# Reading 64 bytes of each row of the first keys and values from ScalarE's queue, ahead of all loads

## The chip, the cores and the metric

The kernel runs on one core of a Trainium2 chip. The metric is the device time of one execution in microseconds (us); lower is better. A core has five engines that run side by side, each with its own instruction stream: TensorE (PE, with the weight loads shown apart as PEld), VectorE (DVE), ScalarE (ACT), GpSimd (POOL) and SyncE (SP). Transfers between the chip's memory and the core's on-chip memory are made by 16 DMA engines. SP, ACT and POOL can issue them, each into a queue of its own.

## The reference

Three stages follow one another, all in float32 (inputs of 8 batches, 8 heads, 576 positions, 64 channels):

```python
a = softmax(phi, axis=2)                       # (8, 8, 576, 32)
k_m = einsum('bhsm,bhsd->bhmd', a, k)          # keys and values summed
v_m = einsum('bhsm,bhsd->bhmd', a, v)          # into 32 memory rows
attn = softmax(q @ k_m.T / 8)
x = (attn @ v_m), heads side by side           # (4608, 512)

logits = x @ moe_phi                           # (4608, 32): 8 experts x 4 slots
slot_input = softmax(logits, axis=0).T @ x
slot_out[e] = relu(slot_input[e] @ w1[e]) @ w2[e]
y = softmax(logits, axis=1) @ slot_out

h = y @ w_in                                   # (4608, 2048)
out = softplus(h) @ w_out                      # (4608, 512)
```

## The kernel before

The host lays the inputs out so that each load is one transfer over 128 partitions. The keys and values of a batch stand in one array `kv[b]` of 128 rows of 18,432 bytes; `phi[b]` has 128 rows of 4,608 bytes, `q[b]` 128 rows of 8,192 bytes.

The order of the work on every engine is written out ahead of time by a small planner in the kernel (`Flow`): generators yield units of work with an assumed duration and the tokens they need, and the planner lists them in one fixed order per engine. It also puts products of a zero tile (`idle`, line 937) into TensorE's stream wherever it expects TensorE to wait; their number and place are fixed when the program is built, and are not changed by what happens on the chip.

There are three stages in time:

- Attention, batch by batch (until about 125 us): loads of `phi`, `kv`, `q`; softmax over the memory rows (`memory_softmax`, DVE line 443, ACT line 447), transposes (line 465), the sums of keys and values (`memory_kv`, line 510), scores, token softmax, logits.
- The experts (about 125 to 177 us): SP streams in `moe_w1` and `moe_w2` (lines 1038 and 1052, tile `w`), TensorE uses each as it comes (lines 1250 and 1283).
- The last two products (177 us to the end): dense TensorE work (line 1795 above all), with the output stored on the way.

All loads are issued by SP, in one fixed order:

```python
def load_kv(b):                                              # lines 400-411
    n = KV + KVL
    parts = (slice(0, n), slice(n, n + KV)) if b == 0 else (slice(0, n + KV),)
    for i, c in enumerate(parts):
        ...
        nc.sync.dma_start(out=kv_t[b][:, c], in_=kv[b][:, c])    # line 409

def attention_loads():                                       # lines 428-436
    yield from load_phi(0)                                       # line 397
    yield [("D", 0.1)], [], 0
    nc.sync.dma_start(out=mphi..., in_=moe_phi)                  # line 431
    for b in range(B):
        yield from load_kv(b)
        if b + 1 < B:
            yield from load_phi(b + 1)
        yield from load_q(b)
```

So SP's order is phi(0), moe_phi, kv(0) in two parts of 10,240 and 8,192 bytes a row, phi(1), q(0), kv(1), phi(2), q(1), and so on. The loads report to eight completion counters in turn, so that each load waits in SP's stream for the one eight places before it; a load also waits until its place in on-chip memory is free. After the attention loads come the first weights `wi`, `wo` of the last stage, the expert weights, and further `wi` and `wo`.

ACT issues no transfer in this kernel. Its stream begins with the loading of an activation table (line 337), and its first computing instruction is the exponential of line 447.

Of the kernel before, what the change touches and what calls it, by code (L numbers as in the profile page):

```python
# [10 lines left out]
F32 = mybir.dt.float32  # L11
# [267 lines left out]
def tile_slot_attention_soft_moe_softplus_mlp(  # L279
# [13 lines left out]
    nc = tc.nc  # L293
# [28 lines left out]
    const = ctx.enter_context(tc.tile_pool(name="const", bufs=1))  # L322
# [11 lines left out]
    SX = room[:, :1152].rearrange("p (k s) -> p k s", k=KC)  # L334
    c_all = room[:, 1152:].rearrange("p (c s) -> p c s", s=NS)

    nc.scalar.preload_act_table_set("natural_log_exp_and_others")
    make_identity(nc, ident)

# [1660 lines left out]
```

## Time and profile before

| | |
|---|---|
| median of 3 runs | 575.95 us (573.95 to 576.41) |
| the profiled execution | 574.74 us |
| its span, first to last instruction | 573.0 us |
| mean granted TensorE clock | 0.997 |
| moved by DMA | 133.63 MB, mean 233 GB/s |

The profile is taken in one execution. Its span leaves 1.74 us of that execution's time outside. The busy time of an engine is an average over stages with different limits, so the rows below are taken by stage. A chain of waits is followed back from the last instruction to whatever released it. In rows on windows, an engine's busy time is in us with the number of instructions, the granted clock is a share of full speed, and DMA share is the busy share of the 16 DMA engines.

### The profile page before, as it was taken

The page shows a single profiled execution, that of the slowest core. Times are in us where ns is not written, and L with a number is a line of the kernel's source. Part 1 is how long each engine was busy: PE and PEld are TensorE (multiplying, and loading weights), DVE is VectorE, ACT ScalarE, POOL GpSimd, SP SyncE. Part 2 cuts the span into 40 slices and gives each one's busy share as a digit, 9 for nine tenths or more (in the row PEclk, how much of TensorE's full clock was granted, in tenths as well). Part 3 has the DMA queues.
Part 4 walks back from the last instruction along what each step waited for, and adds up shares of the span by engine and source line. Part 5 has one row for each costly group of instructions (what it writes and reads, how often), then busy time and mean ns, then how long its engine had stood idle before and what let it go on. Part 6 is the DMA issues. An engine that isn't in the chain of part 4 may idle for free.

```text
span 573.0 us, 10068 instructions
## 1 busy us (share of the span) xinstructions
PE 544.8 (95%) x4039; PEld 415.8 (73%) x4046; DVE 449.8 (79%) x568; ACT 372.9 (65%) x527; POOL 89.7 (16%) x107
## 2 busy tenths in 40 slices
PE   8888998889879999999999999999999999999997
PEld 4566764445536788888788888887888878888885
DVE  3677865749835999999999999999989837787953
ACT  3677674433433797588969876877796976775520
POOL 1021212410000011001032121231212310211100
PEclk9999999999999999999999999999999999999999
DMA  8999999999999458467778975899578774665832
GB/s 314 422 418 424 414 420 428 421 428 415 426 416 420 191 143 226 163 187 172 253 184 158 154 131 98 152 165 172 103 134 148 128 134 69 116 114 114 165 82 110
DMA packets 25103, 133.63 MB, mean 233 GB/s; under 512 B 3296, under 2 KB 4960, under 8 KB 18784
## 3 DMA queue, kind: packets, MB, share of 16 engines
q1 hardware_dynamic: 15120, 96.81, 42.0%
q0 software_dynamic: 9936, 36.18, 36.5%
q8 instruction: 32, 0.52, 0.4%
q14 instruction: 15, 0.12, 0.1%
HBM read 85.00 MB, written 44.04 MB: 225 GB/s over the span
## 4 chain that ended last, share of the span: by engine, by line
PE 84%; DVE 6%; DMA 5%; ACT 3%; issue 1%; POOL 0%; SPq 0%; POOLq 0%; DVEq 0%; ACTq 0%
PE ob L1795 52%; PE ob L1655 8%; DMA w<-in_moe_w_dram 5%; PE hp L1682 5%; PE idle L937 3%; PE kvp L510 3%; PE hid L1250 2%; PE rp L590 1%; PE sc L629 1%; PE tp L465 1%; DVE s L636 1%; PE S L1283 1%; DVE smx L634 1%; PE ob L1823 1%; ACT a L609 1%
## 5 line engine op out<-in xcount | busy, mean ns | idle before, releaser
L1795 PE MATMUL ob<-g,WS 128*128 128x512 f32 x768 | 181.2, 389 | 0.0
L1795 PEld LDWEIGHTS ob<-g,WS 128*128 128x128 f32 x768 | 144.1, 188 | 30.1 <-issue 0.2
L1795 PE MATMUL ob<-g,W 128*128 128x512 f32 x552 | 130.7, 390 | 1.5 <-ACT outs L818 1.3
L1795 PEld LDWEIGHTS ob<-g,W 128*128 128x128 f32 x552 | 103.4, 188 | 24.1 <-ACT outs L818 2.7
L818 ACT ACTIVATE outs<-ob 128x1024 f32<-128x1024 f32 x81 | 83.1, 1026 | 56.1 <-PE ob L1795 47.7
L1444 POOL DMA_DIRECT2D out_dram<-outs x63 | 57.2, 935 | 330.7 <-DVE outs L1437 101.2
L1748 DVE TENSOR_TENSOR g<-arena,g 128x1024 fp32r<-128x1024 f32 x55 | 66.6, 1221 | 26.3 <-ACT g L1746 26.1
L1746 ACT ACTIVATE g<-arena 128x1024 fp32r<-128x1024 f32 x55 | 58.0, 1056 | 17.1 <-PE ob L1795 12.8
L1655 PE MATMUL ob<-g,W 128*128 128x512 f32 x192 | 46.9, 391 | 0.2 <-ACT outs L818 0.2
L1655 PEld LDWEIGHTS ob<-g,W 128*128 128x128 f32 x192 | 35.8, 188 | 8.2 <-ACT outs L818 0.6
L1748 DVE TENSOR_TENSOR g<-room,g 128x1024 fp32r<-128x1024 f32 x29 | 35.2, 1221 | 5.0 <-ACT g L1746 4.8
L1682 PE MATMUL hp<-CT,Gs 128*128 128x512 f32 x128 | 38.3, 390 | 0.0
L1437 DVE TENSOR_TENSOR outs<-ob,outs 128x1024 f32<-128x1024 f32 x27 | 33.0, 1222 | 6.2 <-PE ob L1795 6.0
L1748 DVE TENSOR_TENSOR g<-x,g 128x1024 fp32r<-128x1024 f32 x28 | 34.0, 1220 | 4.8 <-ACT g L1746 4.7
L1746 ACT ACTIVATE g<-room 128x1024 fp32r<-128x1024 f32 x29 | 30.4, 1056 | 4.8 <-PE ob L1795 4.8
L1746 ACT ACTIVATE g<-x 128x1024 fp32r<-128x1024 f32 x28 | 29.6, 1056 | 3.9 <-PE ob L1795 2.3
L937 PE MATMUL idle<-zero 128*128 128x512 bf16 x96 | 26.5, 413 | 2.3 <-POOL zero L940 1.5
L683 POOL TENSOR_TENSOR a<-s,ssm 128x512 f32<-128x512 f32 (+1 forms) x20 | 18.8, 961 | 62.5 <-DVE r L482 24.3
L1695 ACT ACTIVATE arena<-hp 128x1024 f32<-128x1024 f32 x28 | 27.4, 1018 | 1.3 <-DVE g L1748 1.3
L1682 PEld LDWEIGHTS hp<-CT,Gs 128*128 128x128 f32 x128 | 23.9, 188 | 5.3 <-DVE gq L1386 0.2
L1283 PE MATMUL S<-w,hT 128*32 128x256 f32 x256 | 15.8, 381 | 4.2 <-ACT hT L1269 2.1
L510 PE MATMUL kvp<-kv,et 128*32 128x128 f32 x512 | 19.1, 283 | 0.7 <-DMA kv<-in_kv_dram 0.7
(197 smaller groups left out, 734.3 us busy)
## 6 DMA issues: line engine op xcount, KB each, us to landing
out_dram<-outs POOLq DMA_DIRECT2D x63, 512.0 KB, 5.4
w<-in_moe_w_dram SPq DMA_DIRECT2D x15, 2048.0 KB, 18.1
kv<-in_kv_dram SPq DMA_DIRECT2D x7, 2304.0 KB, 25.2
out_dram<-outs SPq DMA_DIRECT2D x20, 512.0 KB, 3.9
q<-in_q_dram SPq DMA_DIRECT2D x8, 1024.0 KB, 21.6
wi<-in_w_in_dram SPq DMA_DIRECT2D x8, 1024.0 KB, 19.0
wo<-in_w_out_dram SPq DMA_DIRECT2D x8, 1024.0 KB, 15.3
phi<-in_phi_dram SPq DMA_DIRECT2D x8, 576.0 KB, 19.5
```

The lines of the kernel that those rows point to most:

```text
L510: nc.tensor.matmul(kvp[32 * h : 32 * h + 32], lhsT=rows[:, 32 * h : 32 * h + 32], rhs=rows_of[:, c, h] if c < SC else rest[:, h], start=(c ...
L818: nc.scalar.activation(o, i, AF.Copy)
L937: nc.tensor.matmul(idle[0], lhsT=zero[:, :128], rhs=zero, start=True, stop=True)
L1283: nc.tensor.matmul(S2[half][32 * i : 32 * i + 32], lhsT=hT_t[e][:, kc8 % 2, kc8 // 2], rhs=w2_t[e, kb][:, half, i], start=(n == 0), stop=( ...
L1437: nc.vector.tensor_tensor(out=o, in0=OB[at], in1=o, op=ALU.add)
L1444: nc.gpsimd.dma_start(out=place(half, tb), in_=o, accum_op=ALU.add)
L1655: nc.tensor.matmul(bank(oc), lhsT=W[u][:, w, i, c], rhs=hb[tb, u][:, x, i], start=(fresh and i == chunks[0] and k == "0"), stop=(stop and ...
L1682: nc.tensor.matmul(hp[:, i], lhsT=Gs[:, 128 * fc : 128 * fc + 128], rhs=CTf[:, TB * tb : TB * tb + TB], start=True, stop=True,)
L1695: nc.scalar.activation(X[key][:, m], hp, AF.Softplus)
L1746: nc.scalar.activation(g[:, 0], x, AF.Copy)
L1748: nc.vector.tensor_tensor(out=g[:, 1], in0=x, in1=g.bitcast(F32)[:, 0], op=ALU.subtract)
L1795: nc.tensor.matmul(OB[at][:, t], lhsT=(W if w == "W" else WS)[u][:, x, c, cols], rhs=g[:, y, m], start=(fresh and u == grp[0] and n == 0), ...
```

## The change

A tile of 64 bytes a partition is added, and ACT's first instruction becomes a transfer that reads the first 64 bytes of each of the 128 rows of `kv[0]` into it. Nothing reads the tile. It stands in front of the table load in ACT's stream. Tiles placed after it in on-chip memory move up by 64 bytes. The transfer takes its turn on the eight completion counters, ahead of SP's loads.

```diff
@@ -334,6 +334,8 @@
     SX = room[:, :1152].rearrange("p (k s) -> p k s", k=KC)
     c_all = room[:, 1152:].rearrange("p (c s) -> p c s", s=NS)
 
+    touched = const.tile([128, 16], F32, name="touched")
+    nc.scalar.dma_start(out=touched, in_=kv[0][:, :16])
     nc.scalar.preload_act_table_set("natural_log_exp_and_others")
     make_identity(nc, ident)
```

## Rows read from the trace of the kernel before

**Rows 1.** The page: busy time of the engines, and the chain that ended last.

```profile
PE 544.8 (95%) x4039; PEld 415.8 (73%) x4046; DVE 449.8 (79%) x568; ACT 372.9 (65%) x527; POOL 89.7 (16%) x107
...
PE 84%; DVE 6%; DMA 5%; ACT 3%; issue 1%; POOL 0%; SPq 0%; POOLq 0%; DVEq 0%; ACTq 0%
```

**Rows 2.** Windows from the first transfer to the last expert weight.

```profile
core 0: us, PE busy (x) PEld busy (x) DVE busy (x) ACT busy (x) POOL busy (x), PEclk, DMA share, GB/s
...
1.70:2.50 0.80, 0.80 (x3) 0.30 (x2) 0.72 (x2) 0.32 (x1) 0.80 (x4) 1.00 0.89 230
2.50:3.60 1.10, 1.10 (x4) 0.33 (x3) 1.09 (x2) 0.00 (x0) 0.81 (x1) 1.00 0.99 377
3.60:7.20 3.60, 3.60 (x11) 1.29 (x10) 1.81 (x4) 1.56 (x4) 0.00 (x0) 1.00 0.90 246
7.20:12.00 4.80, 4.80 (x26) 2.52 (x25) 0.50 (x3) 0.35 (x2) 0.00 (x0) 1.00 0.98 410
12.00:60.00 48.00, 42.44 (x745) 30.16 (x745) 33.94 (x59) 32.19 (x82) 7.41 (x8) 0.96 1.01 422
...
100.00:147.00 47.00, 42.91 (x550) 23.78 (x550) 35.16 (x75) 19.03 (x44) 7.44 (x9) 1.00 1.00 422
147.00:173.00 26.00, 19.48 (x263) 10.46 (x268) 14.28 (x22) 9.63 (x20) 0.00 (x0) 1.00 1.00 421
```

**Rows 3.** The chain of waits, 140 to 180 us: start, us, what.

```profile
147.05 28.23 DMA w<-in_moe_w_dram
...
175.33 0.64 PE S L1283 x8
```

**Rows 4.** TensorE's waits, 150 to 176 us: us in total, times, longest.

```profile
PE S L1283 <- DMA w<-in_moe_w_dram: 2.0, 3, 0.7
PE hid L1250 <- DMA w<-in_moe_w_dram: 1.2, 2, 0.9
```

**Rows 5.** TensorE's waits, 176 us to the end.

```profile
PE ob L1795 <- ACT outs L818: 1.3, 2, 1.1
PE ob L1655 <- ACT outs L818: 0.2, 1, 0.2
```

**Rows 6.** The timeline of the start: start, us, engine, line, operation.

```profile
0.74 1.28 ACT L337 ACT_TABLE_LOAD   x1 [0.74 <-PEq L1984]
...
0.75 0.37 SPq L397 DMA_DIRECT2D phi<-in_phi_dram  x1
...
1.47 9.77 PE L937 MATMUL idle<-zero 128*128 128x512 bf16 x32 [1.47 <-POOL zero L940]
1.65 0.91 SPq L409 DMA_DIRECT2D kv<-in_kv_dram  x2
...
3.56 1.54 SPq L409 DMA_DIRECT2D kv<-in_kv_dram  x1
...
4.25 1.35 DVE L443 TENSOR_REDUCE nmx<-phi 128x2 f32<-128x1152 f32 x1 [0.16 <-DMA phi<-in_phi_dram]
5.14 0.62 SPq L397 DMA_DIRECT2D phi<-in_phi_dram  x1
...
6.41 0.76 ACT L447 ACTIVATE phi<-phi,nmx 128x576 f32<-128x576 f32 x1
...
11.07 0.60 PE L465 MATMUL tp<-ident,phi 128*128 128x128 f32 x4
...
12.47 0.65 PE L510 MATMUL kvp<-kv,et 128*32 128x128 f32 x16
```

**Rows 7.** DMA issues in the first 30 us: count, KB each, us to landing.

```profile
kv<-in_kv_dram SPq DMA_DIRECT2D x1, 1280.0 KB, 8.4
...
mphi<-in_moe_phi_dram SPq DMA_DIRECT2D x1, 64.0 KB, 3.2
```

## Prediction

> **What bounds the kernel now.** I read the page first, then the windows by stage, then the chain of waits around the place where the stages meet, and last the timeline of the first microseconds, where the change acts.
>
> The page makes it look like a TensorE kernel: TensorE is busy 95% of the span and holds 84% of the chain that ended last, the transfers only 5% [rows 1]. That 5% is one piece: the chain goes through a transfer of expert weights that was issued at 147.05 us and landed 28.23 us later, and the product of line 1283 that waited for it starts at 175.33 us [rows 3]. Before that moment the stage is bound by the DMA engines. From 12 us to 173 us their share is 1.00 to 1.01 at 421 to 422 GB/s in every window shown [rows 2]: the queue never runs dry, and the last expert weight lands when all bytes ahead of it have been moved, whenever they were issued. TensorE's high busy time in the first 60 us includes products of a zero tile (line 937) and hides this. From 150 to 176 us TensorE waits five times for weights, 2.0 + 1.2 = 3.2 us in total [rows 4]; it is ready before they are. After 176 us it waits 1.3 + 0.2 = 1.5 us in all, for ScalarE [rows 5]; it is the bound to the end.
>
> So a microsecond gained or lost in the DMA stream anywhere before 175 us arrives at the end nearly whole, up to about the 3.2 us that TensorE has in hand, and one gained on another engine in the start arrives nowhere.
>
> The stream does not start at its full rate. Against 421 GB/s, the windows lose: 1.7 to 2.5 us at 230 GB/s, 0.8 × (1 − 230/421) = 0.36 us; 2.5 to 3.6 us at 377, 0.11 us; 3.6 to 7.2 us at 246, 1.50 us; 7.2 to 12 us at 410, 0.13 us [rows 2]. The sum is 2.1 us. The large term is the third. By bytes, the windows up to 3.6 us have moved 0.18 + 0.41 = 0.60 MB, which is phi(0) (128 × 4,608 bytes = 0.59 MB); moe_phi is 0.07 MB; so from 3.6 us on the stream is in the first part of kv(0). The DMA engines are not idle there (share 0.90): they are slow at what they do.
>
> **The change part by part.**
>
> *The issue on ACT.* SP's issues at the start take 0.37 us to 1.54 us for one transfer [rows 6]. ACT's will take something between, most likely 0.4, and the table load of 1.28 us behind it then ends near 0.74 + 0.4 + 1.28 = 2.4 us, at the latest 0.74 + 1.54 + 1.28 = 3.6 us. What is queued behind it is the exponential of phi(0), which waits for the maximum that VectorE begins at 4.25 us and needs 1.35 us for [rows 6]. The cover is 2.0 us even in the worst case; cost 0. Without that cover, ACT would be late by the difference, and then TensorE's transposes of line 465.
>
> *The transfer itself.* It moves 128 pieces of 64 bytes, 8 KB. At the stream's rate that is 0.02 us. No row shows pieces this small; the nearest is moe_phi, 128 pieces of 512 bytes, 64 KB, 3.2 us from issue to landing [rows 7], whose bytes take 0.16 us of the stream at 421 GB/s. I take 0.05 us between them, nearer the row than the bytes alone would be; both ends stay.
>
> *Its effect on phi(0).* Both are issued near 0.75 us, so the first rows of phi(0) share the DMA engines with it. If phi(0) is later, the maximum of 4.25 us and the exponentials (the second ends at 6.41 + 0.76 = 7.2 us) are later. TensorE comes to phi(0) at 11.07 us, after 32 zero products that it runs in any case [rows 6]. The cover is 3.9 us. Cost 0 in this chain.
>
> *Its effect on kv(0).* The first product on it starts at 12.47 us [rows 6]; the first part was issued at 1.65 us and landed 8.4 us later, at 10.05 us [rows 7]. An earlier landing is worth nothing to TensorE, a later one up to 2.4 us costs it nothing. What counts is the stream behind: kv(0) at full rate lets every later byte go earlier. This is the one term with weight. From below: nothing, if the slow 3.6 us have nothing to do with these rows being read for the first time, or if the small pieces are as slow and hold the same DMA engines. From above: the 1.50 us of the third window. For a gain speaks that phi(0) had just run at 377 GB/s when kv(0) began at 246: the stream was already up, and fell again at this array [rows 2]. Against it speaks that new rows of the same array (kv(0) needs 0.66 + 1.31 = 1.97 MB from the start for its first part, and only about 1.48 MB were moved by 7.2 us), and then q(0), kv(1) and all weights, run at 410 to 422 GB/s at their first reading [rows 2]. A price that is paid once for a stretch of the array, and not by each row, fits both. I take half of the bound, 0.75 us.
>
> In the stream that makes −0.75 + 0.05 = −0.70 us.
>
> The Trainium skill bears on the half (DMA: Bandwidth & Descriptors, section "Issuing engines are not separate DMA queues"): it says that transfers started by different engines run on the same 16 DMA engines and interleave, so a queue of its own saves only issue time. By it ScalarE's queue is no way around: a piece that is slow occupies an engine that phi(0) needs, and the sum would be near +0.05 us. The window that would agree, phi(0) beside another queue, is not in this trace.
>
> *The counters and the addresses.* With the new transfer first in turn, SP's eighth load, phi(2), has it as predecessor. It was issued at 5.14 us [rows 6]; if the new transfer lands by the 3.2 us of moe_phi [rows 7], at 0.75 + 3.2 = 3.95 us, nothing waits. If it were 1.5 us later, phi(2) would be issued 0.3 us late behind kv(1), whose own 2.4 MB need 5.6 us of stream: 0. The shift by 64 bytes changes no instruction; no row prices it, and I take 0 and keep a small chance for new waits (below).
>
> **The sum.** Profiled execution: 574.74 − 0.70 = 574.04 us. That execution lay 1.21 us under the median of the runs, within their spread; on the median it is 575.95 − 0.70 = 575.25, say 575.2 us.
>
> **The rivals.**
>
> *Nothing moves* (0.33). The slow 3.6 us belong to the start of the stream, or their price is paid by the small pieces on the same DMA engines just before. For it: full rate at the first reading of everything later. Against it: the fall from 377 to 246 [rows 2]. Time: 575.95 + 0.02 to 0.16, so 576.0 us. The Trainium skill has a rule that would put the slowness down to load (same page, section "Latency and other measured facts": a memory access takes 0.2 us on average and 2 us at high load). By it a reading at the quiet start would prepare nothing, and the time is this rival's. The trace speaks against it in so far as the load is higher after 12 us, where the rate is full.
>
> *The price is paid twice* (0.14, the other side). The pieces are the first on the DMA engines and as slow as kv(0) is in rows 2, so phi(0) stands behind them for up to 1.50 us, and what 64 bytes prepare does not hold for the other 18,368 of a row. Price: 1.50 + 0.16 = 1.66 us, 577.6 us. It decides as soon as the delay before phi(0) is larger than what is saved after 3.6 us. Against it: phi(0) is itself a first reading, and lost only 0.36 us.
>
> *The whole start is mended* (0.10). All 1.50 us of the third window and the 0.36 us of the first go: 575.95 − 1.86 = 574.1 us.
>
> *Something else moves* (0.08): a new wait from shifted addresses, or TensorE's clock. It was granted 0.96 on average from 12 to 60 us [rows 2], where the stream covers it; half of these cases to each side.
>
> **How the numbers follow.** The forecast, a gain of 0.3 to 1.2 us, has 0.35; it is the likeliest, at 575.2 us. The medians of three runs scatter too: the three shown span 2.5 us. The cases reach from 574.1 to 577.6 us; I leave out the ends of the outer two and add the scatter: 573.6 to 577.3 us. A measurement of this kernel tells about 0.5%, 2.9 us, from no change. The whole slow start is worth 2.1 us and the price paid twice 1.66 us, so no case but the last reaches that by itself; scatter adds a little. Faster 0.07, same 0.86, slower 0.07.
>
> **What would show it.** In the profile after: the window 3.6 to 7.2 us well over 246 GB/s with 1.7 to 3.6 us not lower by as much; kv(0) landing under 8.4 us; the last product of line 1283 starting at about 174.6 instead of 175.33 us; and the span shorter by the same amount. If the first windows lose what the third gains, the first rival holds. If line 1283 starts earlier and the span does not shorten, my step from 175 us to the end is wrong. A new wait in front of the exponential at line 447, or of SP's loads, would make the covers wrong.

## The result, and the profile after

The changed kernel takes 581.43 us (median of 7 runs, 578.24 to 583.85); the kernel before took 575.11 us in the same comparison (7 runs, 573.69 to 578.27). The ratio is 1.0094, 95% interval 1.0069 to 1.0118: slower by about 0.9%. The profiled execution took 581.61 us with a span of 579.8 us and a mean granted clock of 0.985, against 573.0 us and 0.997 before. Lines after the edit are two higher than before (1795 is now 1797).

First the start, where the change acts. This is the timeline of the profile after (start, duration, engine, line, instruction, what released it):

```profile
0.74 0.40 ACTq L338 DMA_DIRECT2D touched<-in_kv_dram  x1
...
1.18 1.28 ACT L339 ACT_TABLE_LOAD   x1 [1.18 <-PEq L1986]
...
4.64 1.35 DVE L445 TENSOR_REDUCE nmx<-phi 128x2 f32<-128x1152 f32 x1 [0.56 <-DMA phi<-in_phi_dram]
...
10.87 0.60 PE L467 MATMUL tp<-ident,phi 128*128 128x128 f32 x4
```

ScalarE's issue takes 0.40 us, the table load ends at 2.46 us, the maximum of phi(0) begins 0.39 us later than before (4.64 for 4.25), and TensorE comes to phi(0) at 10.87 us, and came at 11.07 [rows 6]. Both covers hold. These are the DMA issues of the profile after in the first 30 us (tile, queue, KB, us from issue to landing):

```profile
kv<-in_kv_dram SPq DMA_DIRECT2D x1, 1280.0 KB, 7.7
...
touched<-in_kv_dram ACTq DMA_DIRECT2D x1, 8.0 KB, 4.1
```

The 8 KB take 4.1 us to land, the first part of kv(0) lands in 7.7 us where it took 8.4 [rows 7]. The windows of the profile after, as in rows 2 (busy time of the engines with instruction counts, granted clock, DMA share, GB/s):

```profile
core 0: us, PE busy (x) PEld busy (x) DVE busy (x) ACT busy (x) POOL busy (x), PEclk, DMA share, GB/s
1.70:2.50 0.80, 0.80 (x3) 0.29 (x2) 0.71 (x2) 0.76 (x1) 0.80 (x4) 1.00 0.72 139
2.50:3.60 1.10, 1.10 (x4) 0.32 (x3) 1.09 (x2) 0.00 (x0) 0.81 (x1) 1.00 0.95 374
3.60:7.20 3.60, 3.60 (x11) 1.30 (x10) 1.81 (x4) 1.17 (x3) 0.00 (x0) 1.00 1.05 410
...
12.00:60.00 48.00, 42.79 (x725) 30.02 (x727) 32.33 (x56) 32.16 (x82) 7.41 (x8) 0.93 1.01 424
60.00:100.00 40.00, 35.98 (x594) 23.94 (x586) 24.87 (x56) 24.23 (x62) 9.32 (x11) 0.91 1.02 425
100.00:147.00 47.00, 42.96 (x537) 23.76 (x543) 36.08 (x77) 18.95 (x46) 7.44 (x9) 1.00 0.92 381
147.00:173.00 26.00, 21.08 (x277) 11.48 (x271) 16.61 (x25) 10.94 (x21) 0.00 (x0) 0.93 1.00 421
...
173.00:580.00 407.00, 401.12 (x1886) 324.55 (x1884) 335.78 (x337) 283.65 (x312) 62.32 (x69) 1.00 0.70 156
```

The third window runs at 410 GB/s where it had 246 [rows 2]; the first falls from 230 to 139. Rate times length over the three windows gives 2.00 MB by 7.2 us against 1.48 before: 0.5 MB, 1.2 us of the stream at 421 GB/s. So at the start the transfer does what the forecast hoped for. Two other things are in these windows: the clock is at 0.93, 0.91 and 0.93 in three of them, and from 100 to 147 us the DMA share is 0.92 at 381 GB/s, a stretch in which it was 1.00 at 422.

The chain of waits of the profile after (start, us, engine, line, count):

```profile
174.04 3.80 PE S L1285 x64
177.84 1.26 PE sop L1309 x8
...
216.38 11.19 PE ob L1797 x48
...
300.63 10.99 PE ob L1797 x48
...
507.04 63.21 PE ob L1797 x276
```

No transfer is in it any more. And these are rows of the chain of the kernel before that rows 3 does not show:

```profile
214.06 10.88 PE ob L1795 x48
...
296.51 10.88 PE ob L1795 x48
...
500.85 62.56 PE ob L1795 x276
```

The 6.8 us of longer span have two parts. The product `sop` (line 1309, 1307 before) is the first after the experts. It starts at 177.84 us, and at 175.97 before (175.33 + 0.64, [rows 3]): 1.87 us late. From there to the end before took 573.0 − 175.97 = 397.0 us, and after 579.8 − 177.84 = 402.0: 4.9 us more, in a stretch where the change has no instruction and where the clock is granted at 1.00. The chain shows how it grew: 276 products in a row took 62.56 us, 226.7 ns each, and now 63.21, 229.0 ns each; of two runs of 48 in a row, both at 226.7 ns each, one has 233.1 now and the other 229.0. The costliest group of instructions, after and before:

```profile
L1797 PE MATMUL ob<-g,WS 128*128 128x512 f32 x768 | 183.6, 393 | 0.0
...
L1795 PE MATMUL ob<-g,WS 128*128 128x512 f32 x768 | 181.2, 389 | 0.0
```

These 768 products hold 183.6 us where they held 181.2 (393 ns for 389, by modelled ends); ScalarE's evictions (line 820, 818 before) take 1,026 ns each in both. Nor is it waiting. These are TensorE's waits behind 178 us after the change:

```profile
PE ob L1797 <- ACT outs L820: 1.5, 3, 1.1
PE ob L1657 <- ACT outs L820: 0.2, 1, 0.2
```

That is 1.7 us in all, and it was 1.5 [rows 5].

### The profile page after: what moved, and what is told of

Read it like the earlier page. It is cut to its first block, busy times and chain, and to the rows that moved or that the text cites. A ratio compares the mean times of both kernels' runs of the same rounds, so it can differ in the third digit from the quotient of the medians.

```text
span 579.8 us, 10069 instructions
## 1 busy us (share of the span) xinstructions
PE 554.5 (96%) x4039; PEld 418.4 (72%) x4046; DVE 450.3 (78%) x568; ACT 373.3 (64%) x527; POOL 89.2 (15%) x107
## 4 chain that ended last, share of the span: by engine, by line
PE 83%; DVE 10%; ACT 4%; issue 2%; POOL 0%; DVEq 0%; POOLq 0%; ACTq 0%
PE ob L1797 53%; PE ob L1657 8%; PE hp L1684 5%; PE idle L939 3%; PE kvp L512 2%; PE rp L592 2%; PE tp L467 1%; PE sc L631 1%; DVE s L638 1%; DVE smx L636 1%; PE ob L1825 1%; ACT a L611 1%; PE U L842 1%; DVE arena L1159 1%; PE tp L695 1%
## 5 line engine op out<-in xcount | busy, mean ns | idle before, releaser
L1797 PE MATMUL ob<-g,WS 128*128 128x512 f32 x768 | 183.6, 393 | 0.0
L1797 PE MATMUL ob<-g,W 128*128 128x512 f32 x552 | 132.5, 394 | 1.5 <-ACT outs L820 1.5
L820 ACT ACTIVATE outs<-ob 128x1024 f32<-128x1024 f32 x81 | 83.1, 1026 | 59.6 <-PE ob L1797 50.8
L1657 PE MATMUL ob<-g,W 128*128 128x512 f32 x192 | 47.3, 394 | 0.2 <-ACT outs L820 0.2
L636 DVE TENSOR_REDUCE smx<-sc 128x16 f32<-128x512 f32 (+1 forms) x20 | 12.6, 631 | 9.8 <-PE sc L631 9.8
L939 PEld LDWEIGHTS <-zero 128*128 128x128 bf16 x103 | 10.1, 104 | 12.9 <-issue 4.8
```

The source lines that it names most:

```text
L636: nc.vector.tensor_reduce(out=mx[:, cc], in_=sc[:, : len(cs)], op=ALU.max, axis=AX.X)
L820: nc.scalar.activation(o, i, AF.Copy)
L939: nc.tensor.matmul(idle[0], lhsT=zero[:, :128], rhs=zero, start=True, stop=True)
L1657: nc.tensor.matmul(bank(oc), lhsT=W[u][:, w, i, c], rhs=hb[tb, u][:, x, i], start=(fresh and i == chunks[0] and k == "0"), stop=(stop and ...
L1797: nc.tensor.matmul(OB[at][:, t], lhsT=(W if w == "W" else WS)[u][:, x, c, cols], rhs=g[:, y, m], start=(fresh and u == grp[0] and n == 0), ...
```

## The experiments

Three theories stand in the expectations. A, the *addresses*: `touched` moves tiles behind it by 64 bytes, and some operand is read more slowly there. B, the *transfer*: the early 8 KB set off another order or a late arrival. C, the use of *ScalarE's queue*, which expects what B does except in e4. Beside them stands the *clock*, 0.985 of the whole; it can account for nothing behind 180 us, where all the profiles, of every kernel here, show 1.00. Ratios are to the kernel before, on the same chip, with 95% intervals; "last stretch" is the span from the start of `sop` to the end in the profiled run.

### The shift and the transfer, apart

*e1: the tile alone, with no transfer.*

```diff
+    touched = const.tile([128, 16], F32, name="touched")
```

> The tile of 64 bytes is allocated and nothing is read into it: every tile placed after it lies 64 bytes higher, the transfer is gone. Theory A (addresses): the dense products of the last stage, which step by 229 to 233 ns after the change and by 226.7 ns before, are slow because of where their operands lie; then this kernel is as slow there as the changed one, about 402 us from the last expert product to the end instead of 397, and about 580 us in all. Theory B (the transfer): the early reading of kv(0) is what makes the whole run slower; then this kernel is like the one before, 573 to 577 us, with the window 3.6 to 7.2 us near 246 GB/s. Theory C (the use of ScalarE's queue) expects the same as B.

580.79 us, ratio 1.0108 (1.0081 to 1.0135). `sop` starts at 175.34 us and the last stretch is 402.5 us. The chain of e1:

```profile
175.34 1.26 PE sop L1308 x8
...
504.90 63.21 PE ob L1796 x276
```

An unused tile of 64 bytes, which no instruction touches, costs all of the slow-down, with the 63.21 us of the changed kernel and at a granted clock of 0.994.

*e2: the transfer alone, into the last 64 bytes of a tile that exists and is not yet in use, so that no address moves.*

```diff
+    nc.scalar.dma_start(out=room[:, 2288:], in_=kv[0][:, :16])
```

> The same transfer on ScalarE's queue, into the last 64 bytes of a tile that the kernel has and fills much later, so that no address moves. Theory A (addresses): the start is mended (window 3.6 to 7.2 us near 410 GB/s), the dense products step by 226.7 ns, and the time is 573 to 576 us, up to 1.3 us less than before. Theory B (the transfer) and theory C (ScalarE's queue): about 581 us, as after the change.

575.67 us, ratio 1.0008 (0.9986 to 1.0029). The last stretch is 396.9 us again. Its chain:

```profile
179.43 1.26 PE sop L1308 x8
...
504.26 62.56 PE ob L1796 x276
```

The 62.56 us of before are back. `sop` comes at 179.43 us in this profile, at a clock of 0.982; this is the second part, taken up below.

*e3: the change with a tile of 256 bytes, of which the transfer fills the first 64.*

```diff
-    touched = const.tile([128, 16], F32, name="touched")
-    nc.scalar.dma_start(out=touched, in_=kv[0][:, :16])
+    touched = const.tile([128, 64], F32, name="touched")
+    nc.scalar.dma_start(out=touched[:, :16], in_=kv[0][:, :16])
```

> The change with a tile of 256 bytes instead of 64: the tiles after it move by 256 bytes, the transfer is the same. Theory A (addresses) with a dependence on the place within 256 bytes: fast, 573 to 576 us; with any other dependence it may be slow too. Theories B and C: about 581 us.

575.41 us, ratio 1.0013 (0.9995 to 1.0032); 62.56 us for the 276 products, last stretch 396.8. Moved by 256 bytes the operands give the step of before; moved by 64 they do not.

*e4: the transfer of e2, as the first on SP's queue.*

```diff
+    nc.sync.dma_start(out=room[:, 2288:], in_=kv[0][:, :16])
```

> The same transfer of 64 bytes a row as the first one of SP's queue, ahead of phi(0), into the existing tile, so that no address moves and ScalarE issues nothing. Theory A (addresses): fast, 573 to 576 us, with the start mended. Theory B (the transfer): about 581 us. Theory C (ScalarE's queue): fast, 573 to 577 us.

574.93 us, ratio 1.0001 (0.9982 to 1.0021); last stretch 396.9 us. The windows of e4:

```profile
1.70:2.50 0.80, 0.80 (x3) 0.30 (x2) 0.71 (x2) 0.33 (x1) 0.80 (x4) 1.00 0.64 91
2.50:3.60 1.10, 1.10 (x5) 0.33 (x3) 1.09 (x2) 0.00 (x0) 0.82 (x1) 1.00 0.80 218
3.60:7.20 3.60, 3.60 (x16) 1.55 (x15) 1.82 (x4) 0.71 (x2) 0.00 (x0) 1.00 1.03 402
```

The third window is mended from SP's queue as well. But the new transfer now stands ahead of phi(0) in SP's stream, and the first two windows are lower than in e2 (168 and 376 GB/s): 1.76 MB by 7.2 us, for 1.92 in e2.

### Which address

In the built program of the kernel before, the operands of the dense products all stand at 224 modulo 256: the weights `W` and `WS` on one side of on-chip memory, `CT`, `Gs` and four of the six tiles `g` on the other. The two remaining tiles `g` lie on the weights' side and come into use late, at about 440 us; 96 of the last 276 products of line 1795 read them. The change moves the tiles of the second side alone, so four of the six `g` move against their weights. `CT` and `Gs`, moving operand and weights of line 1682, move together. So it could be where `g` stands by itself, or how far it is from the weights, or another tile altogether.

*e5: no transfer; 64 bytes directly ahead of the four tiles `g` (and the small `gq` behind them), all else in its place.*

```diff
+    pad = wp.tile([128, 16], F32, name="pad")
```

> No transfer. 64 unused bytes are put directly in front of the tiles g alone, the moving operand of the dense products (and of the small tile gq behind them); everything else lies as in the kernel before. Theory A1 (the place of the moving operand decides): as slow as the run with all tiles 64 bytes higher, dense products at 229 to 233 ns, ratio 1.008 to 1.013. Theory A2 (another of the moved tiles decides, such as the outputs that ScalarE and VectorE write, or the tiles they read): as before, 226.7 ns and ratio 0.998 to 1.003.

580.26 us, ratio 1.0089 (1.0063 to 1.0115); last stretch 401.4 us, 276 products in 63.22 us. The tile that matters most is `g`, the moving operand of lines 1655 and 1795: 4.4 us of the 5.5 that e1 loses in the last stretch.

*e6: 64 bytes ahead of everything, as in e1, and 192 more ahead of `g`, so that `g` alone is back.*

```diff
+    pad = const.tile([128, 16], F32, name="pad")
...
+    pad = wp.tile([128, 48], F32, name="pad")
```

> No transfer. All tiles behind the constants lie 64 bytes higher, and 192 unused bytes in front of the tiles g put these at 256 bytes above their old place, which the run with 256 bytes showed to be harmless. Theory A1 (the moving operand): 226.7 ns and ratio 0.998 to 1.003. Theory A2 (another tile): 229 to 233 ns, ratio 1.008 to 1.013.

576.74 us, ratio 1.0031 (1.0009 to 1.0053); 62.61 us for the 276 products, last stretch 399.2. The last 276 products are nearly back, and more than half of the loss is gone. Still moved by 64 in e6 are all other tiles of that side, `CT` and `Gs` among them. Rows of its chain tell where the 2.2 us that are left lie:

```profile
213.54 10.93 PE ob L1797 x48
...
249.92 2.77 PE ob L1797 x12
```

In the kernel before, such runs take 10.88 and 2.72 us. A run of 12 products, of 48 or of 276 is longer by the same 0.05 us: the first products after a change from line 1684 to line 1797 are slower, the others not. `CT` and `Gs` have kept their distance from each other, but not from `g` and its weights. That a product is held up by the weights of its neighbour would fit; no run shows it.

*e7 and e8: everything behind the constants on the side of `g` moved by 32, and by 128 bytes.*

```diff
+    pad = const.tile([128, 8], F32, name="pad")      # e7
+    pad = const.tile([128, 32], F32, name="pad")     # e8
```

> No transfer. All tiles behind the constants lie 32 bytes higher, so that the tiles g start at a multiple of 256 bytes (before: 32 bytes below one). Theory A1: if what counts is how a row of the moving operand stands to a boundary, this one is the best place there is: 226.7 ns or less, ratio at most 1.00. If any move from the old place costs, it is slow like the 64 bytes: ratio 1.008 to 1.013.

> No transfer. All tiles behind the constants lie 128 bytes higher. Theory A with a period of 128 bytes: as before, 226.7 ns, ratio 0.998 to 1.003. Theory A with a period of 256 bytes: slow, ratio over 1.005.

e7: 585.21 us, ratio 1.0172 (1.0154 to 1.0191). e8: 583.29 us, ratio 1.0142 (1.0119 to 1.0165). Both are worse than 64 bytes.

*e9: the weights 64 bytes lower, by a pad at the top of their side; four of the six tiles `g` and all of `CT` and `Gs` stay.*

```diff
+    low = ctx.enter_context(tc.tile_pool(name="low", bufs=1, side="right"))
+    pad_r = low.tile([128, 16], F32, name="pad_r")
```

> No transfer. The other side of the memory is moved: 64 unused bytes at its top put all weights W and WS of the dense products 64 bytes lower, and four of the six tiles g stay where they were. Theory A1a (what counts is where the moving operand lies against the weights, within 256 bytes): slow, 228 to 233 ns, ratio 1.007 to 1.018. Theory A1b (what counts is the place of the moving operand alone, which has not moved for those four): as before, 226.7 ns and ratio 0.997 to 1.003.

580.74 us, ratio 1.0096 (1.0058 to 1.0133); last stretch 402.5 us. Its chain:

```profile
506.38 63.21 PE ob L1797 x276
```

So it is not the place of `g` by itself: with `g` unmoved and the weights moved the 63.21 us of e1 are there again.

*e10: the pad of e9, and 192 bytes ahead of everything on the left: all operands at 160 modulo 256, the same distances as before.*

```diff
+    pad = const.tile([128, 48], F32, name="pad")
...
+    low = ctx.enter_context(tc.tile_pool(name="low", bufs=1, side="right"))
+    pad_r = low.tile([128, 16], F32, name="pad_r")
```

> No transfer. 64 unused bytes at the top and 192 behind the constants: every operand of the dense products lies at another place within 256 bytes than before (160 instead of 224), and all of them at the same. Theory A1a (against the weights): as before, 226.7 ns and ratio 0.997 to 1.003. Theory A1b (the place alone): slow, ratio over 1.005.

575.08 us, ratio 0.9991 (0.9975 to 1.0007); last stretch 396.9 us. Its chain:

```profile
500.50 62.56 PE ob L1798 x276
```

No operand of the dense products stands where it did, and the time is that of before. With e9 this shows the distance (A1a in the expectations): the moving operand against the weights, modulo 256 (256 more, in e3 and e10, costs nothing; other multiples were not tried).

*e11 and e12: the four tiles `g` alone moved, as in e5, by 96 and by 192 bytes.*

```diff
+    pad = wp.tile([128, 24], F32, name="pad")        # e11
+    pad = wp.tile([128, 48], F32, name="pad")        # e12
```

> No transfer. 96 unused bytes directly in front of the tiles g alone. Theory A1a: slow, ratio 1.005 to 1.018, by an amount that is not known beforehand (32 bytes cost 1.7%, 64 bytes 0.9 to 1.1%, 128 bytes 1.4%). If only some distances from the weights cost and others gain, it could be under 1.00.

> No transfer. 192 unused bytes directly in front of the tiles g alone, which is 64 bytes short of 256. Theory A1a: slow, ratio 1.005 to 1.018, and if the distance counts the same in both directions, near the 1.009 of 64 bytes. A ratio under 0.998 would make it a better place than the one before.

e11: 584.45 us, ratio 1.0159 (1.0137 to 1.018). e12: 583.62 us, ratio 1.0148 (1.0124 to 1.0171). The same run of 48 in the chains of e7, e8, e11 and e12, in this order:

```profile
301.03 11.19 PE ob L1796 x48
...
298.71 11.16 PE ob L1796 x48
...
300.65 11.20 PE ob L1796 x48
...
299.35 11.19 PE ob L1796 x48
```

Together, by the distance of the four moved `g` from the weights modulo 256 (a step is a row of that kernel's chain over its products; in the run of 48 every product has the distance named, in the last 276 the 96 on the two other tiles `g` are at distance 0 in every kernel, so that this column is a mixture):

| distance | kernels | step in the 48 near 300 us | step in the last 276 products | last stretch | ratio |
|---|---|---|---|---|---|
| 0 | before, e2, e3, e4, e10 | 226.7 ns | 226.7 ns | 396.8 to 397.0 us | 0.9991 to 1.0013 |
| 32 | e7 | 233.1 ns | 231.5 ns | 406.1 us | 1.0172 |
| 64 | after, e1, e5, e9 | 228.8 to 229.2 ns | 229.0 ns | 401.4 to 402.5 us | 1.0089 to 1.0108 |
| 96 | e11 | 233.3 ns | 231.7 ns | 406.5 us | 1.0159 |
| 128 | e8 | 232.5 ns | 231.2 ns | 405.4 us | 1.0142 |
| 192 | e12 | 233.1 ns | 231.3 ns | 405.9 us | 1.0148 |

64 is the mildest that was tried. It is not symmetric: 192, which is 64 to the other side, costs as much as 128. Nor is the distance of `g` all: in the other run of 48, near 215 us, the changed kernel, e1 and e9 have 233.1 to 233.3 ns at distance 64 and e5 has 229.2. What else decides there is open.

### What mends the start of the stream

Kernels without a transfer ahead (before, and e1 and e5 to e12) have 246 to 288 GB/s in the window from 3.6 to 7.2 us; the changed kernel and e2 to e4 have 380 to 415. By the three windows, the former have moved 1.48 to 1.66 MB by 7.2 us, on average 1.6; the changed kernel, e2 and e3 1.9 to 2.0, and e4 1.76. The forecast put the slow third window down to a first reading of these rows. Three single runs with other addresses, on the edit of e2:

*e13 reads the queries, e15 the keys and values of another batch, e14 only 16 of the 128 rows.*

```diff
+    nc.scalar.dma_start(out=room[:, 2288:], in_=q[0][:, :16])          # e13
+    nc.scalar.dma_start(out=room[:16, 2288:], in_=kv[0][:16, :16])     # e14
+    nc.scalar.dma_start(out=room[:, 2288:], in_=kv[4][:, :16])         # e15
```

> A transfer of the same form on ScalarE's queue, into the existing tile, reads 64 bytes of each row of q(0) instead of kv(0). Theory F (the rows of kv(0) are slow because they are read for the first time, and an earlier reading pays that price beside phi(0)): the window 3.6 to 7.2 us stays slow, 230 to 300 GB/s as without a transfer. Theory G (any small transfer ahead mends the start, whatever it reads): 380 to 415 GB/s, as with kv(0).

> The transfer on ScalarE's queue reads 64 bytes of the first 16 rows of kv(0) only, not of all 128. Theory F with a price per row: window 3.6 to 7.2 us slow, near 250 to 300 GB/s, seven eighths of the price being left. Theory F with a price per larger stretch of the array: mended in part, 300 to 380. Theory G: 380 to 415 GB/s.

> The transfer on ScalarE's queue reads 64 bytes of each row of kv(4), 9.4 MB further on in the same array. Theory F with a price for rows or stretches: window 3.6 to 7.2 us slow, 230 to 300 GB/s. A price for the array as a whole, and theory G: 380 to 415 GB/s.

574.19, 574.83 and 575.99 us, with 575.01 for the kernel before beside them; one run each, so the times tell nothing apart. The windows do. The third window of e1, which has no transfer:

```profile
3.60:7.20 3.60, 3.60 (x10) 1.33 (x9) 1.81 (x4) 1.62 (x4) 0.00 (x0) 1.00 0.91 286
```

The same window of e2, which reads kv(0):

```profile
3.60:7.20 3.60, 3.60 (x13) 1.47 (x12) 1.81 (x4) 1.28 (x3) 0.00 (x0) 1.00 0.99 380
```

Of e13, which reads the queries:

```profile
3.60:7.20 3.60, 3.60 (x13) 1.40 (x12) 1.81 (x4) 1.13 (x3) 0.00 (x0) 1.00 1.04 392
```

Of e14, with 16 rows:

```profile
3.60:7.20 3.60, 3.60 (x15) 1.54 (x14) 1.81 (x4) 1.41 (x3) 0.00 (x0) 1.00 0.96 311
```

Of e15, which reads another batch:

```profile
3.60:7.20 3.60, 3.60 (x15) 1.49 (x14) 1.81 (x4) 1.28 (x3) 0.00 (x0) 1.00 1.02 392
```

Reading `q` or a batch that is not needed for a long time mends kv(0) as well as reading kv(0) itself: 392 GB/s. So it is not a price on those rows (G in the expectations: any small transfer ahead does it). Sixteen pieces do little of it, 311 GB/s and 1.68 MB by 7.2 us. Why a small transfer ahead helps is open.

## Why the prediction was wrong

The forecast was 575.2 us in a range of 573.6 to 577.3, with 0.07 for slower. It came out 6.3 us longer than before, outside the range.

**The step that failed** is the one on the addresses: "The shift by 64 bytes changes no instruction; no row prices it, and I take 0". It changes no instruction and yet the duration of over a thousand of them: of the 1,536 products of lines 1797 (768 + 552), 1657 (192) and 1825 (24), 1,332 read one of the four moved `g`. 4.9 us over these are 3.7 ns each on average, between the 2.3 and 6.4 ns of the two runs of 48 (line 1684's products have a small part in it). e1 shows that the shift alone does it; e5, e9 and e10 show through which operands. A rival ("something else moves") did name shifted addresses, at 0.08 together with the clock and half to each side, but looked for a new wait; there is none, and the products themselves became longer.

What an honest bound would have been: no row of before shows operands at another distance, so the cost of the edit had no upper end from rows, on the stretch where TensorE is the bound for 397 us. One per cent of it is 4 us, more than all other terms together. The prediction gave this the same 0 as the counters.

The Trainium skill (SBUF — State Buffer, section "Who interferes with whom") says that TensorE has two independent read ports, one for the moving operand and one for the weights, and that only the port pair shared by VectorE and GpSimd causes contention. Read by that alone, no address would cost anything; of addresses the section says nothing. The measurements differ: 226.7 ns at distance 0, and 228.8 to 233.3 in runs of 48 at all others, with the same work. They do not show what it is in the memory or in TensorE that makes the difference.

**The transfer** was right in size at the start. The third window is mended, and 0.5 MB or 1.2 us of stream are gained against the profile before (whose 246 GB/s is the lowest of all kernels without a transfer; against their average of 1.6 MB by 7.2 us it is 0.4 MB, about 1.0 us). The forecast had −0.75 + 0.05. The reason was wrong: not a first reading of those rows (e13, e15). The rule that the prediction weighed against it, that transfers of any engine share the same DMA engines (the Trainium skill, DMA: Bandwidth & Descriptors, section "Issuing engines are not separate DMA queues"), agrees with e4, where SP's queue mends the third window as well, and with the first window's fall from 230 to 139; but the sum that was drawn from it, near +0.05 us, did not come at the start of the stream.

**That it arrives at the end** held only half. The step was that a microsecond of stream before 175 us arrives at the end nearly whole, with 3.2 us in TensorE's hand. That margin is what TensorE's lateness used up. The clock goes with it: `sop` starts at 175.97 us with a mean clock of 0.997 (before), at 177.84 with 0.985 (after), at 179.43 and 179.31 with 0.982 (e2, e3). Of the signs that the prediction named, the third window and the landing of kv(0) came, and the earlier start of line 1283's last product did not. TensorE's waits from 150 to 178 us in the profile after:

```profile
PE S L1285 <- ACT hT L1271: 2.1, 2, 1.0
PE ctp L1222 <- DVE c L1216: 1.6, 1, 1.6
```

There were waits for weights here [rows 4]; now there are none, since TensorE itself is late, and `sop` comes 1.87 us later although the stream started better. The stream itself did not stay full, which the step took for granted. The load of expert weights that SP issues at 130.38 us before, and the windows around it, before and after:

```profile
130.38 0.33 SPq L1038 DMA_DIRECT2D w<-in_moe_w_dram  x1
...
130.00:135.00 5.00, 5.00 (x74) 2.79 (x70) 4.87 (x7) 2.39 (x7) 0.00 (x0) 1.00 0.97 400
```

```profile
133.82 0.33 SPq L1040 DMA_DIRECT2D w<-in_moe_w_dram  x1
...
130.00:135.00 5.00, 4.35 (x57) 2.15 (x59) 4.34 (x9) 0.56 (x2) 0.00 (x0) 1.00 0.35 103
```

The load is issued 3.44 us later, in both kernels behind a wait for TensorE, which is late by then, and the queue runs low: 103 GB/s for 400. From 100 to 147 us, 381 for 422 GB/s costs (1 − 381/422) × 47 = 4.6 us of stream, more than the start had gained. A mean clock of 0.985 means 2 × 0.015 × 579.8 = 17 us at the lower of TensorE's levels, 1.2 for 2.4 GHz, against 3.4 us before. It lies ahead of 173 us; from there to the end the window shows 1.00.

How often, the repeated runs tell. Of 29 runs of the kernel before (beside e1 to e4), 26 had a clock of 0.989 or more, with a median of 574.86 us; the other 3 had 579.74. Of e2's 12 runs, 6 stood at 0.990 or more, with a median of 574.2 us, and 6 at 0.982 to 0.987, with 577.4; e3 had 6 (574.1) and 6 (577.9); e4 had 11 (574.90) and 1 (578.61). Of the kernels without a transfer, e1 and e5 to e12, 8 of 50 runs lay below 0.989. So at the higher clock the transfer on ScalarE's queue is worth 0.6 to 0.8 us, near what the sum said (an indication: medians of six runs each, picked by their clock; e4, whose first two windows are lower, shows no gain), and in half of its runs the lower clock takes 3 to 4 us back: hence 1.0008 and 1.0013 instead of 0.999. The changed kernel adds both: three of its seven runs at 0.991 or more took 578.2 to 579.9 us, the others 581.4 to 583.9.

Why the clock falls more often was not settled. One place stands out in the profiles. These are the windows from 24 us on of the changed kernel:

```profile
24.00:26.00 2.00, 1.15 (x8) 0.58 (x8) 2.00 (x3) 1.85 (x5) 0.00 (x0) 1.00 1.05 442
26.00:28.00 2.00, 1.87 (x21) 0.60 (x20) 1.86 (x6) 1.69 (x6) 0.57 (x1) 0.76 1.00 424
28.00:31.00 3.00, 2.24 (x46) 1.29 (x39) 0.50 (x1) 1.08 (x2) 1.48 (x2) 0.50 0.93 388
```

And the same windows of the kernel before:

```profile
24.00:26.00 2.00, 1.43 (x28) 0.85 (x19) 2.00 (x4) 1.85 (x3) 0.00 (x0) 1.00 1.12 458
26.00:28.00 2.00, 1.87 (x22) 0.60 (x20) 1.86 (x6) 1.87 (x7) 0.38 (x1) 1.00 0.96 397
28.00:31.00 3.00, 2.07 (x48) 1.77 (x47) 0.69 (x1) 1.10 (x3) 1.67 (x2) 1.00 1.03 436
```

TensorE is busy 1.15 of 2 us with 8 products, where it was 1.43 with 28, and then the clock goes to 0.50. TensorE finishes the earlier work sooner, since kv(1) lands sooner (its products begin at 21.38 us, before at 22.13), while the `idle` products keep the number and order that were written out when the program was built. e3's profile shows the same fall at the same place. Against the argument stand e2, with 10 products in 1.10 us from 24 to 26 us and a clock of 1.00 in all three windows (it falls elsewhere), and e7, without a transfer, whose products on kv(1) begin late, at 22.85 us, and whose clock falls as well:

```profile
24.00:26.00 2.00, 2.00 (x47) 2.00 (x43) 1.25 (x2) 0.59 (x1) 0.00 (x0) 0.50 1.12 461
```

e11, also without one, has the same. The kernel before falls too, between 31 and 60 us (0.94). So the cause of the falls is not shown.

**The covers** held: ACT's issue, phi(0), the counters (phi(2) is issued at 4.82 us, before at 5.14). No load waits for the new transfer, though it took 4.1 us to land where the estimate was 3.2.

No kernel that was tried beats the kernel before by more than a measurement can tell.

## What to carry to other kernels

An edit that allocates on-chip memory can move the operands of later stages; ask how far a moving operand then stands from its weights before calling it free, and undo the move (a pad to a full 256 bytes, or a place in an existing tile) before judging the rest of the edit. Where a stage of dense products sets the end, a per-product change of 1% outweighs anything won in the first microseconds. And a gain at the start reaches the end only if the engine that it feeds keeps its pace on the way: look at the granted clock of repeated runs, not of one profile.

## What was not expected of the hardware

- Products of 128 x 512 in a row start every 226.7 ns when the moving operand and the weights stand at the same place modulo 256 bytes, and every 232.3 to 233.3 ns in runs of 48 at a distance of 32, 96, 128 or 192; at 64 it is 228.8 to 229.2 in one run and up to 233.3 in another. Over this kernel that is 0.9 to 1.7%.
- The first large load runs at 246 to 288 GB/s for its first 3.6 us, and at 380 to 415 when 8 KB in 128 pieces go ahead (they read three places: kv(0), another batch, the queries), from ScalarE's queue or SP's; with 16 pieces it is 311.
- The first transfer of 8 KB takes 4.1 us from issue to landing.
